# Reordering two small pieces of a matmul-bound kernel: a PSUM copy ahead of a gelu, and weight sums made form by form

## The chip, the cores and the metric

The kernel runs on one core of a Trainium2 chip. The metric is device time in microseconds (us), lower is better. The trace is one execution, taken by the hardware profiler; its span is about 1.7 us shorter than the time that is measured for the same execution.

Engines: PE is TensorE's matmul, PEld its weight load, DVE is VectorE, ACT is ScalarE, POOL is GpSimd, SP here only issues DMAs. PSUM is the memory in whose banks the matmuls accumulate. The granted clock is the share of TensorE's full clock that the trace records (1.00 is full, 0.50 is half). `L927` is line 927 of the kernel that the profile belongs to.

## The reference

```python
x = A_x                                             # 2048 x 1024
g = sigmoid((x * gate_w).sum(-1, keepdims=True))
a = A_ref(x, A_wqkv, A_wo)      # 32 heads of 32; each query sees 8 keys, at distance 0, 2, .. 14
b = B_ref(x, w_gate, w_up, w_down)                  # (gelu(x w_gate) * (x w_up)) w_down, 3584 wide
return g * a + (1 - g) * b
```

All arrays are bf16. `gelu` is the tanh approximation.

Of the kernel before, what the change touches and what calls it, by code (L numbers as in the profile page):

```python
# [136 lines left out]
def kernel(  # L137
# [19 lines left out]
    KH = KT // 2  # L157
# [55 lines left out]
    def tt(n, f32=False):  # L213
        return 0.07 + n / (960.0 if f32 else 1920.0)
# [25 lines left out]
    def ring_take(key):  # L240
        held[key] = ring_free.pop(0)[0]
        return ring[:, held[key], :]
# [278 lines left out]
    def qkv_forms():  # L521
        for sup in range(1, NSUP):
            c = 2 * sup
            t = tt(D // 2)
            for which in range(3):
                def g3(key):
                    return ring[:, held[key], :].rearrange("p (m t) -> p m t", t=NT)

                def raw(kt, hi, which=which, c=c):
                    return g3(("wqkv", c, which, kt))[:, :, KH * hi:KH * hi + KH]  # L530

                def form(f, kt, which=which, c=c):
                    return ring[:, held["wqf", c, which, f, kt // 2], kt % 2 * D // 2:(kt % 2 + 1) * D // 2] \
                        .rearrange("p (m t) -> p m t", t=KH)

                for k0 in range(0, KH, 2):
                    for f in (0, 2, 1, 3):
                        for kt in (k0, k0 + 1):
                            def go(f=f, kt=kt, which=which, c=c):
                                if f != 2 and kt % 2 == 0:  # L540
                                    ring_take(("wqf", c, which, f, kt // 2))
                                o, x_, y_, op = ((lambda: form(0, kt), lambda: raw(kt, 1), lambda: raw(kt + KH, 1), ALU.add),
                                                 (lambda: form(1, kt), lambda: form(0, kt), lambda: raw(kt, 0), ALU.subtract),
                                                 (lambda: raw(kt, 1), lambda: raw(kt, 0), lambda: raw(kt, 1), ALU.subtract),
                                                 (lambda: form(3, kt), lambda: raw(kt + KH, 0), lambda: form(1, kt),
                                                  ALU.subtract))[f]
                                V(out=o(), in0=x_(), in1=y_(), op=op)  # L547
                            dep = [("wqkv", c, which, kt), ("wqkv", c, which, kt + KH)]
                            if f in (1, 2):
                                dep.append(("wq", c, which, 0, kt))  # L550
                            elif f == 3:
                                dep.append(("wq", c, which, 1, kt))
                            yield dve(t, go, dep, key=("wq", c, which, f, kt), lag=0.5,
                                      pre=ring_pre if (f != 2 and kt % 2 == 0) else None)
# [365 lines left out]
    def ffn(sup, mid):  # L920
        T3, B22, B11, B21 = xr[:, 0], xr[:, 1], xr[:, 2], xr[:, 3]
        T1, T2, T4 = tf[:, 0], tf[:, 1], tf[:, 2]

        def mm(bk, form, rhs, f, start):
            wv, fl = piece(("w", sup, f // FB, form), KH), f % FB
            for k in range(KH):
                nc.tensor.matmul(banks[bk][:], lhsT=wv[:, k, fl * P:(fl + 1) * P], rhs=rhs[:, k, :],  # L927
                                 start=(start and k == 0), stop=(k == KH - 1), skip_group_check=True)

        def prod(bk, form, rhs, f, start, deps):  # L930
            b = f // FB
            o = pe(KH, lambda: mm(bk, form, rhs, f, start), [("w", sup, b, form)] + [x_ for x_ in deps if x_ is not None])
            yield o
            if f % FB == FB - 1:
                if sup == 0 and NSUP > 1 and not isinstance(form, str):
                    ring_give(("w", sup, b, form), o, w.done[("ws", b, form)])
                else:
                    ring_give(("w", sup, b, form), o)
            return o

        A, Bk, Dk, m5, u2, gl, ev = {}, {}, {}, {}, {}, {}, {}
        xf = [("xf", sup)]

        def hs(f, half):
            return hT[:, (1 - half) * NST:(2 - half) * NST, f, :]

        def v3(ap):
            return ap.rearrange("p (j s) -> p j s", s=P)

        for i in range(FT + 2):  # L950
            if i < FT:
                f = i
                A[f], fr = bank_take()
                o = yield from prod(A[f], "A11", B11, f, True, [fr] + xf)
                Bk[f], fr = bank_take()
                ev[f, "seed"] = act(0.5, lambda f=f: nc.scalar.copy(out=banks[Bk[f]][:], in_=banks[A[f]][:]), [o, fr] if fr else [o])  # L956
                yield ev[f, "seed"]
            if i >= FT:
                yield from mid[i - FT]
            if i >= 2:  # L960
                f = i - 2
                o = yield from prod(Bk[f], "A22", T4, f, False, [ev[f, "up2"]])
                e = act(0.48, lambda f=f: nc.scalar.copy(out=hs(f, 0), in_=v3(banks[Bk[f]][:])), [o])  # L963
                yield e
                bank_give(Bk[f], e)
                yield dve(tt(2 * SC), lambda f=f: nc.vector.tensor_tensor(  # L966
                    out=hT[:, :, f, :], in0=hT[:, :, f, :], in1=gl[f][:].rearrange("p (j s) -> p j s", s=P), op=ALU.mult),
                    [e, ev[f, "g1"], ev[f, "g2"]], key=("h", sup, f))
            if i < FT:
                f = i  # L970
                Dk[f], fr = bank_take()
                o = yield from prod(Dk[f], 0, T1, f, True, [fr])

                def cp(f=f):
                    m5[f] = work.tile([P, SC], F32, tag="m5", bufs=2, name="m5")
                    nc.scalar.copy(out=m5[f][:], in_=banks[Dk[f]][:])
                ev[f, "m5"] = act(0.48, cp, [o])
                yield ev[f, "m5"]
            if 1 <= i < FT + 1:
                f = i - 1  # L980
                o = yield from prod(Bk[f], 2, T3, f, False, [ev[f, "u2"]])
                d = [("stored", "o")] if (sup == 0 and f >= 8) else []
                if sup and f >= FT - NT:
                    d = [("qkv", 2 * sup + 1, 0, 0)]
                ev[f, "up2"] = dve(tt(SC, True), lambda f=f: nc.vector.tensor_tensor(
                    out=hs(f, 1), in0=v3(banks[Bk[f]][:]), in1=v3(m5[f][:]), op=ALU.add), [o, ev[f, "m5"]] + d)
                yield ev[f, "up2"]
            if i < FT:
                f = i
                o = yield from prod(A[f], "A12", B21, f, False, [ev[f, "seed"]])  # L990

                def g1(f=f):
                    gl[f] = work.tile([P, 2 * SC], BF16, tag="gl", bufs=3, name="gl")
                    nc.scalar.activation(out=gl[f][:, SC:2 * SC], in_=banks[A[f]][:], func=ACT.Gelu_apprx_tanh)  # L994
                ev[f, "g1"] = act(0.52, g1, [o], table="gelu")
                yield ev[f, "g1"]
                bank_give(A[f], ev[f, "g1"])
                o = yield from prod(Bk[f], 1, T2, f, False, [ev[f, "seed"]])

                def cp2(f=f):  # L1000
                    u2[f] = work.tile([P, SC], F32, tag="u2", bufs=2, name="u2")
                    nc.scalar.copy(out=u2[f][:], in_=banks[Bk[f]][:])  # L1002
                ev[f, "u2"] = act(0.48, cp2, [o])
                yield ev[f, "u2"]
                o = yield from prod(Dk[f], 3, B22, f, False, [ev[f, "m5"]])
                e = dve(tt(SC, True), lambda f=f: nc.vector.tensor_tensor(out=u2[f][:], in0=banks[Dk[f]][:],  # L1006
                                                                          in1=u2[f][:], op=ALU.add), [o, ev[f, "u2"]])
                yield e
                bank_give(Dk[f], e)
                ev[f, "g2"] = act(0.54, lambda f=f: nc.scalar.activation(out=gl[f][:, 0:SC], in_=u2[f][:],  # L1010
                                                                         func=ACT.Gelu_apprx_tanh), [e], table="gelu")
                yield ev[f, "g2"]
        w.done[("ffn", sup)] = o

    def down(c):
# [214 lines left out]
```

## The kernel before: what the change and the argument touch

The matmuls (qkv of the second half, gate/up, down) are made from seven products of half-sized blocks instead of eight (Strassen-Winograd). That needs sums of the weights and of x, made on VectorE ("forms"), and accumulators that are copied from one PSUM bank to another on ScalarE before more products are added to the copy (the "seed").

Instructions are not written in engine order by hand. Several Python generators ("streams") each yield operations in their own order, and a small list scheduler emits, again and again, the head that could start first by its own estimate of costs and of DMA landing times. On each engine, **the order of emission is the order of execution** (the trace before shows what that does: ScalarE stood idle for 3.82 us up to 102.91 before a gelu whose input was late, with the data of the seed copy emitted behind it ready):

```python
def _start(self, op):
    ...
    for d in deps:
        t = max(t, d.end + (0.04 if d.eng == op.eng else self.LAT + op.lag))
    return t
...
w.run([(0.0, main()), (0.0, loads()), (0.1, wforms()), (0.1, x_forms()), (0.1, qkv_forms()),
       (0.15, preps()), (0.3, attention()), (0.5, scores())])   # smallest estimate + bias goes first
```

The gate/up stage, one turn per block f of 128 columns (cut to its PE products and ACT copies, in order):

```python
for i in range(FT + 2):
    A11(i)      -> bank A                       # PE, 4 matmuls each
    seed(i):    bank Bk <- bank A               # ACT copy, L956
    A22(i-2)    -> Bk ; cast hT(i-2) <- Bk      # ACT, L963 ; DVE: hT *= gelu, L966
    form0(i)    -> Dk ; m5(i) <- Dk             # ACT copy, L976
    form2(i-1)  -> Bk ; DVE hT <- Bk + m5       # L985
    A12(i)      -> A  (needs seed(i)) ; g1(i) = gelu(A)     # ACT, L994
    form1(i)    -> Bk ; u2(i) <- Bk             # ACT, L1002
    form3(i)    -> Dk (needs m5(i)) ; DVE u2 <- Dk + u2     # L1006
    g2(i) = gelu(u2)                            # ACT, L1010, then the next turn's A11
```

The sums of the second qkv weights (16 for each of q, k, v; four forms times four row blocks):

```python
for k0 in range(0, KH, 2):          # rows 0,1 first, then rows 2,3
    for f in (0, 2, 1, 3):
        for kt in (k0, k0 + 1):
            yield dve(t, go, dep, key=("wq", c, which, f, kt), lag=0.5, ...)   # L547
```

PE uses them in the order: a product of raw weights, form 0 (all four rows, for two output blocks), form 1, raw, form 2, form 3, raw.

## Time and profile before

| | before |
|---|---|
| time, median of 3 | 745.33 us (744.88 to 747.23) |
| span of the traced execution | 744.5 us |
| PE busy | 727.6 us, 98% |
| DVE busy | 630.8 us, 85% (nearly gapless from 90 to 330) |
| ACT busy | 318.6 us, 43% |

First part of the page of the kernel before: busy us, share of the span, instructions.

```profile
PE 727.6 (98%) x3365; PEld 357.7 (48%) x3365; DVE 630.8 (85%) x931; ACT 318.6 (43%) x535; POOL 71.2 (10%) x123
```

PE is busy 98%, so only PE's waits can be won by moving things. They are few, and a view lists them. Waits of PE in the kernel before: who waited for whom, us in total, times, longest.

```profile
PE ps L580 <- DVE ring L547: 6.2, 2, 5.9
PE ps L927 <- ACT ps L956: 3.5, 3, 2.8
PE ps L274 <- DVE hT L272: 1.2, 1, 1.2
PE ps L1066 <- DMA ring<-in_A_wo_dram: 1.0, 2, 0.6
```

The first line is the weight sums of q, the second the seed copies; these two are what the change is after.

Timeline of the kernel before around the longest seed wait: start us, length, engine, line, operation, then the number of instructions merged into the line, and in brackets the idle time before it and what ended it.

```profile
102.19 0.68 DVE L1006 TENSOR_TENSOR u<-ps,u 128x512 f32<-128x512 f32 x1
...
102.91 0.63 ACT L1010 ACTIVATE gl<-u 128x512 bf16<-128x512 f32 x1 [3.82 <-DVE u L1006]
...
103.44 0.58 ACT L956 COPY ps<-ps 128x512 f32<-128x512 f32 x1
...
104.08 1.02 PE L927 MATMUL ps<-xr,ring 128*128 128x512 bf16 x4 [2.80 <-ACT ps L956]
```

ACT stood idle for 3.82 us with the seed's data ready (its matmuls ended near 99.4), because the gelu stood first in its queue and waited for VectorE, which was in attention work until 102.2.

Timeline of the kernel before, VectorE around the longest wait, with PE's restart last.

```profile
328.15 2.10 DVE L547 TENSOR_TENSOR ring<-ring 128x512 bf16<-128x512 bf16 x6
...
331.00 1.22 DVE L448 TENSOR_TENSOR xr<-xr 128x2048 bf16<-128x2048 bf16 x1
...
332.99 1.22 DVE L449 TENSOR_TENSOR tf<-xr,tf 128x2048 bf16<-128x2048 bf16 x1
334.13 3.10 DVE L547 TENSOR_TENSOR ring<-ring 128x512 bf16<-128x512 bf16 x9
...
334.94 4.76 PE L580 MATMUL ps<-tf,ring 128*128 128x512 bf16 x14 [5.90 <-DVE ring L547]
```

With one that ran at 326.55, seven sums are done by 330.2, but only two of the four rows of form 0 are among them. Two transposes for the gate (L690, 0.71 us each, among the lines left out) and two differences of x (L448, L449) stand before rows 2 and 3. Read also the last line's length: 14 matmuls took 4.76 us, where 216 ns apart they take 3.0 (the spacing of an undisturbed stretch of this trace: 8 in 1.89 us at 326.26, of which the last takes 0.38).

### The profile page before, as it was taken

The numbers are of one execution on the slowest core, as the hardware profiler recorded it, in microseconds if no ns is written. First come the engines' busy times: TensorE is split into PE (matmuls) and PEld (weight loads), VectorE is DVE, ScalarE is ACT, GpSimd is POOL, SyncE is SP. The second block draws the span as 40 slices with busy tenths as digits, with TensorE's granted clock in tenths as the row PEclk, the third lists the DMA queues.
The fourth block names the chain that finished last, engine by engine and source line by source line (L and its number), as shares of the span: only waits on it lengthen the run. The fifth ranks groups of instructions, "written<-read, shape, count | busy, mean of one in ns | idle before, by whom it ended". The sixth has DMA issues, their size and how long they took to land. (4 is left out here: it accounts for less than half of the span.)

```text
span 744.5 us, 9889 instructions
## 1 busy us (share of the span) xinstructions
PE 727.6 (98%) x3365; PEld 357.7 (48%) x3365; DVE 630.8 (85%) x931; ACT 318.6 (43%) x535; POOL 71.2 (10%) x123
## 2 busy tenths in 40 slices
PE   8999989999999999969999999999999999999997
PEld 5666634444444444435655444444444444444443
DVE  2789999999999999996999999999999997894300
ACT  2333445558555561016453121575566556210110
POOL 1234422121212000010000001000000000001000
PEclk9999999999999999999999999999999999999999
DMA  9999955655555459970234999855464645899983
GB/s 305 329 323 361 378 169 155 184 169 181 164 180 176 155 180 326 312 266 28 85 114 142 313 308 327 247 148 162 135 174 125 181 130 170 267 304 327 331 288 122
DMA packets 150435, 162.68 MB, mean 219 GB/s; under 512 B 22896, under 2 KB 110960, under 8 KB 150384
## 3 DMA queue, kind: packets, MB, share of 16 engines
q1 hardware_dynamic: 141552, 134.25, 58.7%
q0 software_dynamic: 8544, 27.27, 10.2%
q8 instruction: 26, 0.43, 0.2%
q10 hardware_dynamic: 288, 0.52, 0.2%
q14 instruction: 25, 0.20, 0.1%
HBM read 129.50 MB, written 28.31 MB: 212 GB/s over the span
## 5 line engine op out<-in xcount | busy, mean ns | idle before, releaser
L927 PEld LDWEIGHTS <-ring 128*128 128x128 bf16 x1568 | 153.4, 98 | 189.4 <-issue 5.1
L927 PE MATMUL ps<-xr,ring 128*128 128x512 bf16 x896 | 213.2, 379 | 3.5 <-ACT ps L956 3.5
L927 PE MATMUL ps<-tf,ring 128*128 128x512 bf16 x672 | 164.0, 379 | 0.0
L1066 PE MATMUL ps<-ring,hT 128*128 128x512 bf16 x708 | 160.6, 379 | 0.0
L1066 PEld LDWEIGHTS <-hT 128*128 128x128 bf16 x708 | 69.2, 98 | 83.5
L740 DVE TENSOR_TENSOR xbuf<-qo,kT 128x2048 bf16<-128x2048 bf16 x64 | 77.2, 1216 | 2.1 <-ACT kT L486 2.1
L879 DVE TENSOR_TENSOR xbuf<-xbuf,vT 128x2048 bf16<-128x2048 bf16 x64 | 77.4, 1217 | 0.2
L746 DVE TENSOR_TENSOR xbuf<-xbuf 128x2048 bf16<-128x2048 bf16 x56 | 68.1, 1216 | 0.2
L580 PEld LDWEIGHTS <-ring 128*128 128x128 bf16 x336 | 44.0, 131 | 36.6 <-DVE ring L547 7.2
L1010 ACT ACTIVATE gl<-u 128x512 bf16<-128x512 f32 x56 | 35.3, 631 | 61.0 <-DVE u L1006 61.0
L1101 ACT ACTIVATE ost<-ps,omg 128x512 bf16<-128x512 f32 x16 | 11.0, 687 | 115.0 <-PE ps L1066 115.0
L464 PE MATMUL ps<-xr,ring 128*128 128x512 bf16 x256 | 55.6, 379 | 0.3 <-DVE xr L1168 0.3
L1093 POOL DMA_DIRECT2D out_dram<-ost x24 | 13.0, 540 | 435.2 <-ACT ost L1101 340.8
L994 ACT ACTIVATE gl<-ps 128x512 bf16<-128x512 f32 x56 | 33.4, 597 | 47.9 <-PE ps L927 46.6
L1066 PE MATMUL ps<-ring,qo 128*128 128x512 bf16 x192 | 49.8, 379 | 1.2 <-DMA ring<-in_A_wo_dram 1.0
L464 PEld LDWEIGHTS <-ring 128*128 128x128 bf16 x256 | 36.7, 144 | 18.8 <-issue 0.4
L1006 DVE TENSOR_TENSOR u<-ps,u 128x512 f32<-128x512 f32 x56 | 38.4, 686 | 6.7 <-PE ps L927 3.6
L966 DVE TENSOR_TENSOR hT<-hT,gl 128x1024 bf16<-128x1024 bf16 x56 | 38.3, 684 | 6.3 <-ACT hT L963 6.1
L580 PE MATMUL ps<-xr,ring 128*128 128x512 bf16 x192 | 43.4, 379 | 0.0
L433 POOL DMA_DIRECT2D fforms<-ring x56 | 30.4, 544 | 126.0 <-DVE ring L425 115.9
L887 DVE TENSOR_TENSOR xbuf<-xbuf 128x1024 bf16<-128x1024 bf16 x64 | 41.8, 684 | 0.4
L580 PE MATMUL ps<-tf,ring 128*128 128x512 bf16 x144 | 35.0, 392 | 6.2 <-DVE ring L547 6.2
(101 smaller groups left out, 735.0 us busy)
## 6 DMA issues: line engine op xcount, KB each, us to landing
ring<-dforms SPq DMA_DIRECT2D x112, 256.0 KB, 4.7
ring<-in_B_w_down_dram SPq DMA_DIRECT2D x84, 256.0 KB, 4.1
ring<-in_B_w_gate_dram SPq DMA_DIRECT2D x56, 256.0 KB, 5.0
fforms<-ring POOLq DMA_DIRECT2D x56, 256.0 KB, 4.2
ring<-fforms SPq DMA_DIRECT2D x56, 256.0 KB, 3.7
ring<-in_B_w_up_dram SPq DMA_DIRECT2D x42, 256.0 KB, 3.9
ring<-in_A_wqkv_dram SPq DMA_DIRECT2D x40, 256.0 KB, 5.8
ring<-oforms SPq DMA_DIRECT2D x32, 256.0 KB, 5.6
```

The costliest lines, as they stand in the source:

```text
L464: nc.tensor.matmul(banks[bk][:], lhsT=lhsT, rhs=xT(c, kt), start=(kt == 0), stop=(kt == KT - 1))
L580: nc.tensor.matmul(banks[bk][:], lhsT=lhsT, rhs=rhs[:, kt, :], start=(start and kt == 0), stop=(kt == KH - 1), skip_group_check=True)
L740: V(out=w3(box[t]), in0=q_b, in1=k_w, op=ALU.mult)
L746: V(out=w3(box[0]), in0=w3(box[0]), in1=w3(box[t]), op=ALU.add)
L879: return dve(tt(n), taking(("p", t), lambda: V(out=w3(box["p", t]), in0=w3(box["ab"]), in1=v_w, op=ALU.mult)), [("qkv", c, 2, t), abo] + ( ...
L887: V(out=s4(t)[:, t % 2], in0=w3(box["p", t])[:, 0:4], in1=w3(box["p", t])[:, 4:8], op=ALU.add)
L927: nc.tensor.matmul(banks[bk][:], lhsT=wv[:, k, fl * P:(fl + 1) * P], rhs=rhs[:, k, :], start=(start and k == 0), stop=(k == KH - 1), skip_ ...
L966: yield dve(tt(2 * SC), lambda f=f: nc.vector.tensor_tensor(out=hT[:, :, f, :], in0=hT[:, :, f, :], in1=gl[f][:].rearrange("p (j s) -> p j ...
L994: nc.scalar.activation(out=gl[f][:, SC:2 * SC], in_=banks[A[f]][:], func=ACT.Gelu_apprx_tanh)
L1006: e = dve(tt(SC, True), lambda f=f: nc.vector.tensor_tensor(out=u2[f][:], in0=banks[Dk[f]][:], in1=u2[f][:], op=ALU.add), [o, ev[f, "u2"]])
L1010: ev[f, "g2"] = act(0.54, lambda f=f: nc.scalar.activation(out=gl[f][:, 0:SC], in_=u2[f][:], func=ACT.Gelu_apprx_tanh), [e], table="gelu")
L1066: nc.tensor.matmul(banks[bk][:], lhsT=l, rhs=wv[:, i, :], start=(start and k == 0), stop=(q == last and i == 1), skip_group_check=True)
```

## The change

Its intent: (1) let the seed of the next turn pass the gelu that waits for VectorE; (2) finish form 0 for all rows before any other form, in the order in which PE uses them. No work is added or removed.

```diff
-                for k0 in range(0, KH, 2):
-                    for f in (0, 2, 1, 3):
-                        for kt in (k0, k0 + 1):
+                for f in range(4):
+                    for kt in range(KH):
+                        if True:
                             def go(f=f, kt=kt, which=which, c=c):
 ...
-        xf = [("xf", sup)]
+        xf, late = [("xf", sup)], []
 ...
                 yield ev[f, "seed"]
+            while late:
+                yield late.pop(0)
             if i >= FT:
 ...
                 ev[f, "g2"] = act(0.54, lambda f=f: nc.scalar.activation(... Gelu_apprx_tanh), [e], table="gelu")
-                yield ev[f, "g2"]
+                late.append(ev[f, "g2"])
```

## The prediction

> What bounds it now. The page's first part gives TensorE (PE) 727.6 of 744.5 us busy, VectorE 631, ScalarE 319. So only PE's waits can be won. The view of PE's waits lists, after the start, 6.2 us for VectorE's sums of qkv weights (two waits, longest 5.9), 3.5 us for ScalarE's seed copies (2.8, 0.5, 0.2) and 1.0 us for a DMA. The rest is launch and tail, untouched.
>
> Seed copy part. It adds and removes nothing: the 631 ns gelu moves behind the next 579 ns seed copy. The timeline shows the 2.8 us wait at 101.3-104.1: VectorE reached the gelu's input only at 102.19, the gelu ran 102.91-103.5, then the seed, although the seed's own matmuls had ended near 99.4. After the change the seed is ready by 100, but the copy of the next product (the m5 buffer), still behind the gelu, ends near 104.1, where PE would need it at 103.0. I expect some 1.1 us of the stall to come back there: 1.7 us won. At 559.9 the 0.5 us wait (gelu behind an exp and two 1.28 us table loads) should vanish whole. The 0.2 us one belongs to a first seed, with no gelu ahead: stays. Side effect: the cast into hT comes up to 0.6 us later where the gelu used to be early; VectorE may idle a little before the multiply with the gelu. It is not bounding except near 324.
>
> Weight sums part. Same 16 sums (417 ns, 350 apart) for each of q, k, v, in another order. Timeline, 326-335: VectorE has been without a gap since about 275. It does seven sums (two rows of forms 0, 2, 1 and one of form 3) by 330.2, then two gate transposes and two 1.22 us differences of x, and only at 334.5-335.3 form 0 of rows 2 and 3, for which PE waits. Putting form 0 of all rows first would seem to remove all 6 us. I don't expect that. VectorE's order is fixed when the program is emitted, on estimated landing times; rows 2 and 3 of the weights are expected later than rows 0 and 1. So I expect row 2's form 0 ahead of the gate's transposes, one attention difference (0.65 us) slipped in before it, and row 3's form 0 still behind the two x differences, near 333.5-334. PE's stall shrinks from 5.9 to about 4.3 us. After today's stall 14 matmuls take 4.76 us instead of 14 x 0.216 = 3.0, at a granted clock of 0.6[...] half of 1.7 us expected. Weights of k and v: PE doesn't wait for them today, and should not after.
>
> Sum: 1.7 + 0.5 + 1.4 + 0.8 = 4.4 us less, provided that VectorE, which waits for PE now and then between 100 and 275, inherits PE's 1.7 us lead; else the second stall grows by it. Prediction 741.2 us, range 738.3 to 744.6. Chances: faster by over 2% 0.02, within 2% 0.96, slower 0.02.
>
> Right if: PE's waits show no seed wait over 0.3 us, one about 1 us wait for the m5 copy or none; the wait for the weight sums is 3-5 us, behind the last x difference; all busy times are unchanged within 0.5%. Wrong if: the weight sum wait disappears (then 736-738), or the forms of k and v become a wait, or a late cast delays VectorE in the first half so that the wait near 330 doesn't shrink (744-746).

The last term, 0.8 us, is the author's estimate: half of the about 1.7 us by which the 14 matmuls after the 5.9 us stall (4.76 us in the trace of the kernel before) exceed 3.0.

## More of the kernel before

The change adds two lines, so lines after 957 move down by two in the changed kernel (the gelu L1010 is L1012 there, the m5 copy L976 is L978).

A load's estimated end is that of a single pipe of 340 GB/s, plus 2.2 us. Both are constants in the scheduler's code (`RATE` and the line that sets a load's end), not measurements; the page of the kernel before has up to 378 GB/s in one of its 20 slices and medians of 3.7 to 5.8 us from issue to landing in the lines that it lists.

## The result, and the profile after

| | before | after |
|---|---|---|
| time, median of 4 | 745.8 us (744.88 to 747.23) | 741.23 us (740.83 to 741.6) |
| span of the traced execution | 744.5 | 739.1 |
| PE waits for seeds | 3.5 us | none listed |
| PE waits for the m5 copy | none | 3.1 us, two of 1.5 |
| PE waits for weight sums | 6.2 us | 1.6 us |

The ratio is 0.9937, 95% interval 0.9919 to 0.9955. Here and below a ratio is the mean time of one kernel's runs over that of the other's of the same rounds, so it is not quite the ratio of the medians. Executions over 1.5% slower than the fastest of the same kernel are left out of the means. The output is correct.

The time is the predicted one to 0.03 us, and the parts are not. Waits of PE in the changed kernel:

```profile
PE ps L927 <- ACT m L978: 3.1, 2, 1.5
PE ps L580 <- DVE ring L547: 1.6, 1, 1.6
PE ps L274 <- DVE hT L272: 1.2, 1, 1.2
```

The seed waits are gone, but nearly as much came back as waits for the m5 copy. Timeline of the changed kernel, the place that answers to 102-104 above:

```profile
100.65 0.57 ACT L956 COPY ps<-ps 128x512 f32<-128x512 f32 x1 [0.55 <-PE ps L927]
...
102.54 0.57 ACT L978 COPY m<-ps 128x512 f32<-128x512 f32 x1
...
102.99 1.03 PE L927 MATMUL ps<-tf,ring 128*128 128x512 bf16 x4
```

The seed now runs at 100.65, as soon as its matmuls end, and PE does not stop. The m5 copy that I expected to be late ends at 103.1, in time: VectorE reached the gelu's input (L1008) 6.1 us after the stage's first matmul (101.29 against 95.21), before the change 8.0 us after it (102.19 against 94.19). This distance isn't the change's doing: two experiments below that keep the old order here (sums_only and filler) have 5.7 and 7.8 us, so it differs between executions, and with it the wait. The two m5 waits lie elsewhere. Timeline of the changed kernel before the first of them, ScalarE alone and, last, PE (the second, at 550, has the same sequence):

```profile
255.79 1.28 ACT L703 ACT_TABLE_LOAD   x1
257.09 0.22 ACT L703 ACTIVATE ez<-zc 128x16 f32<-128x16 f32 x1
257.21 0.58 ACT L956 COPY ps<-ps 128x512 f32<-128x512 f32 x1
257.81 1.28 ACT L1012 ACT_TABLE_LOAD   x1
259.10 0.63 ACT L1012 ACTIVATE gl<-u 128x512 bf16<-128x512 f32 x1
...
260.22 1.28 ACT L838 ACT_TABLE_LOAD   x1
261.52 0.63 ACT L838 ACTIVATE xbuf<-xbuf 128x512 f32<-128x512 f32 x1
262.05 0.57 ACT L978 COPY m<-ps 128x512 f32<-128x512 f32 x1
...
262.67 1.02 PE L927 MATMUL ps<-xr,ring 128*128 128x512 bf16 x4 [1.53 <-ACT m L978]
```

The gelu stands between two exps (the gate's at 257.09 and the attention's at 261.52), so the function table is loaded three times here and, for the gelu after it, once more. A load takes 1283 ns (the mean of each line's), and the whole switch at 255.79 took 1.3 us: the copy before it ended at 255.78, the exp began at 257.09. The m5 copy waits behind all of it. Over the whole kernel the table is loaded 18 times, before 16 times.

Timeline of the changed kernel, VectorE at the weight sums and PE's restart:

```profile
326.17 0.36 DVE L547 TENSOR_TENSOR ring<-ring 128x512 bf16<-128x512 bf16 x1
326.44 0.70 DVE L690 STREAM_TRANSPOSE zt<-ps 128x512 f32<-128x512 f32 x1
...
329.24 1.22 DVE L449 TENSOR_TENSOR tf<-xr,tf 128x2048 bf16<-128x2048 bf16 x1
330.38 4.44 DVE L547 TENSOR_TENSOR ring<-ring 128x512 bf16<-128x512 bf16 x13
...
331.10 2.75 PE L580 MATMUL ps<-tf,ring 128*128 128x512 bf16 x12 [1.60 <-DVE ring L547]
```

The order is the predicted one: row 2's form 0 (326.17) stands before the transposes, row 3's (the first of the 13) behind the last difference of x. But it happens over 3 us earlier than I had put it: row 3's at 330.4, not 333.5 to 334. And the matmuls after the wait are not slow: 12 in 2.75 us. So VectorE reached this place much earlier, though nothing was taken from its work. The experiments had to find which half of the change did that.

### The profile page after: what moved, and what is told of

It is laid out like the page before. It is cut to its first block, busy times and chain, and to the rows that moved or that the text cites. A ratio compares the mean times of both kernels' runs of the same rounds, so it can differ in the third digit from the quotient of the medians.

```text
span 739.1 us, 9823 instructions
## 1 busy us (share of the span) xinstructions
PE 723.0 (98%) x3298; PEld 358.0 (48%) x3365; DVE 630.6 (85%) x931; ACT 321.6 (44%) x537; POOL 71.2 (10%) x123
## 4 chain that ended last, share of the span: by engine, by line
PE 86%; DVE 7%; DMA 2%; ACT 2%; issue 2%; DVEq 0%; ACTq 0%
PE ps L927 44%; PE ps L1068 21%; PE ps L464 11%; PE ps L580 9%; DVE xbuf L879 1%; DMA ring<-dforms 1%; DVE xbuf L887 1%; DVE xbuf L746 1%; DMA ring<-fforms 1%; DVE hT L1036 1%; DVE xbuf L740 0%; DMA hT<-in_A_x_dram 0%; PE ps L685 0%; PE ps L1163 0%; DVE tf L1036 0%
## 5 line engine op out<-in xcount | busy, mean ns | idle before, releaser
L927 PE MATMUL ps<-tf,ring 128*128 128x512 bf16 x659 | 162.6, 379 | 0.8
L956 ACT COPY ps<-ps 128x512 f32<-128x512 f32 x56 | 32.1, 573 | 52.9 <-PE ps L927 52.9
L1008 DVE TENSOR_TENSOR u<-ps,u 128x512 f32<-128x512 f32 x56 | 38.4, 686 | 5.9 <-PE ps L927 2.7
L987 DVE TENSOR_TENSOR hT<-ps,m 128x512 bf16<-128x512 f32 x56 | 38.5, 687 | 3.0 <-PE ps L927 2.6
```

Of the source, the lines that this page charges most:

```text
L927: nc.tensor.matmul(banks[bk][:], lhsT=wv[:, k, fl * P:(fl + 1) * P], rhs=rhs[:, k, :], start=(start and k == 0), stop=(k == KH - 1), skip_ ...
L987: ev[f, "up2"] = dve(tt(SC, True), lambda f=f: nc.vector.tensor_tensor(out=hs(f, 1), in0=v3(banks[Bk[f]][:]), in1=v3(m5[f][:]), op=ALU.add ...
L1008: e = dve(tt(SC, True), lambda f=f: nc.vector.tensor_tensor(out=u2[f][:], in0=banks[Dk[f]][:], in1=u2[f][:], op=ALU.add), [o, ev[f, "u2"]])
```

## Experiments

All results were correct. The first four below ran on one chip, the others on a second. Times are medians of fast runs.

### The two halves alone

The sums' order alone, seeds as before; and the seeds alone, sums' order as before. Each is the diff above with the other half left out. The changed kernel ran again beside them.

> The changed kernel again, beside its two halves. Repeat of 0.9937, 0.992 to 0.996; PE waits 1.6 us for the weight sums and twice 1.5 us for the m5 copy, none for a seed.

> Only the new order of the weight sums. My theory (VectorE stands where it stood before, row 3's form 0 is still behind both x differences, as predicted): seed waits 2.8, 0.5 and 0.2 stay, the sums' wait goes from 5.9 to about 4.3 us, ratio 0.997 to 0.999. Rival A (the order of the sums alone makes the big gain): the wait falls below 2 us and the ratio is at or below 0.995.

> Only the seed copies ahead of the gelu. My theory after seeing the result: no seed wait over 0.3 us, but two new 1.5 us waits for the m5 copy, and VectorE earlier against PE near 325, so the sums' wait falls too, to 2 to 3.5 us, though the sums' order is the old one; ratio 0.994 to 0.997. Rival A: the sums' wait stays near 6 us and the ratio is 0.998 or more.

The last column is PE's time from its first raw product of q to the first product behind form 0, 24 matmuls; without a stop they took 5.18 us (the run `landing` below).

| | median us | ratio to before (95%) | sums' wait | m5 waits | seed waits | PE's form-0 stretch |
|---|---|---|---|---|---|---|
| before (waits and stretch: its trace, as above) | 746.16 | 1 | 6.2 | 0 | 3.5 | 13.27 |
| both (after_again) | 740.45 | 0.9929 (0.9915 to 0.9943) | 2.4 | 3.1 | 0 | 9.39 |
| sums_only | 744.62 | 0.9984 (0.9971 to 0.9997) | 5.2, longest 3.9 | 0 | 1.6 | 13.26 |
| seed_only | 742.64 | 0.9953 (0.9936 to 0.9970) | 3.2 | 3.1 | 0 | 8.67 |

The weight sums' order alone measured 1.5 us (0.2 to 2.2 us by the interval). Its profile has the order that the prediction drew: longest wait 3.9 us (predicted about 4.3), row 3 behind the x differences. But I had expected the seed waits of 2.8, 0.5 and 0.2 us to stay, and that missed. The long one is 0.5 us here, and the restart at the sums is as slow as before. Timeline of sums_only, both places:

```profile
102.56 1.02 PE L927 MATMUL ps<-xr,ring 128*128 128x512 bf16 x4 [0.54 <-ACT ps L956]
...
332.33 5.27 PE L580 MATMUL ps<-tf,ring 128*128 128x512 bf16 x13 [3.86 <-DVE ring L547]
```

Up to the sums VectorE has the same order in both kernels, so the seed wait alone differs by 2.3 us between executions. At the sums nothing was gained in this trace: the stretch took 13.26 us, before 13.27, as slower matmuls followed the shorter stall (13 in 5.27 us). So how much of the 1.5 us the sums' order wins is not shown.

The seeds alone are worth 3.5 us, although their own waits net to almost nothing (3.5 us taken away, 3.1 us of m5 waits put in their place). The gain is at the *other* wait: the sums' wait fell from 6.2 to 3.2 us with the sums' order untouched, and the matmuls behind it kept the full clock, so the stretch took 8.67 us instead of 13.27.

Why? Busy time of each engine between 90 and 320 us, in the kernel before, in sums_only and in seed_only (columns: stretch, its length, then busy us and instructions of PE, PEld, DVE, ACT, POOL, the granted clock, DMA share, GB/s):

```profile
90.00:320.00 230.00, 226.03 (x1045) 102.39 (x1044) 222.41 (x311) 115.82 (x194) 31.58 (x57) 1.00 0.67 201
```

```profile
90.00:320.00 230.00, 228.60 (x1057) 103.91 (x1056) 222.48 (x311) 116.29 (x194) 31.70 (x58) 1.00 0.67 203
```

```profile
90.00:320.00 230.00, 227.19 (x1049) 103.07 (x1048) 224.60 (x314) 116.13 (x194) 32.08 (x58) 1.00 0.67 201
```

The third busy time is VectorE's. With the seeds ahead it does 224.6 us of work in these 230 us, without them 222.4. It waits 2.2 us less. The large transpose of the attention half that precedes the sums (L803) began at 319.4 in sums_only and 315.9 in the changed kernel. Its lines in the kernel before and in seed_only:

```profile
320.88 2.30 DVE L803 STREAM_TRANSPOSE xbuf<-xbuf 128x2048 bf16<-128x2048 bf16 x1
```

```profile
315.42 2.30 DVE L803 STREAM_TRANSPOSE xbuf<-xbuf 128x2048 bf16<-128x2048 bf16 x1
```

The two groups don't overlap: 314.8 to 316.1 in the six usable traces with the gelu moved and the exps (below) left alone, 319.4 to 322.8 in the three with the old order of the seeds (filler is the third). So the seed half moved VectorE ahead by about 5 us at this place. In seed_only it is 5.5 us. VectorE was idle for 27.7 us up to the transpose instead of 31.3; 0.7 of these 3.6 us lie before 62 us, ahead of this stage's first seed (95 us), and are chance. Another 0.7 us is one output operation that now stands behind the transpose. All the other instructions before it are the same in number and kind; they were busy 1.1 us less.

### The slow matmuls after a stall

After the 5.9 us stall of the kernel before, matmuls came 430 ns apart for about 3.3 us. I filled that stall with 20 repeats of one matmul whose result is overwritten.

```diff
                 for kt in range(KH):
 ...
+                    if which == 0 and t == 0 and form == 0 and kt == 0:
+                        for _ in range(20):
+                            nc.tensor.matmul(banks[bk][:], lhsT=lhsT, rhs=rhs[:, kt, :], start=True, stop=False, ...)
```

> The kernel before with 20 repeats of one matmul (4.3 us of PE work, overwritten) put into its 5.9 us stall. If the slow matmuls after the stall (14 in 4.76 us) are the cost of a clock halved by the idle time, the stall's end stays at the same sum and the time falls by 1.5 to 1.9 us: ratio 0.9975 to 0.998. If those matmuls are slow because they wait for the following sums one by one, ratio 0.9995 to 1.0005.

Measured: 744.91 us, ratio 0.9988 (0.9968 to 1.0008), single runs from 743.23 to 748.41. The ratio is inconclusive. In the profile a wait of 2.3 us was left, and after it 14 matmuls took 5.01 us: the clock fell all the same. But this execution is the slowest of the six and the only one with a mean granted clock of 0.995; the others have 0.998 to 1.000, while all 33 executions of the kernel before that ran beside the experiments have 0.993 to 0.995. So the filler kept more of the clock in most executions; the two at 1.000 took 743.23 and 743.74 us.

The changed kernel has 1.000 in six of its ten executions (739.96 to 740.86 us) and 0.997 or 0.998 in four (741.59 to 742.69), seed_only 1.000 in two of six, sums_only in none. So part of the change's gain is a clock that is lost less often. The profiles show single cases. Timeline lines of PE's restart at the sums, in after_again, seed_only and filler:

```profile
331.07 4.64 PE L580 MATMUL ps<-tf,ring 128*128 128x512 bf16 x13 [2.38 <-DVE ring L547]
```

```profile
331.12 3.33 PE L580 MATMUL ps<-tf,ring 128*128 128x512 bf16 x14 [3.18 <-DVE ring L547]
```

```profile
336.81 5.01 PE L584 MATMUL ps<-tf,ring 128*128 128x512 bf16 x14 [2.31 <-DVE ring L547]
```

The mean granted clock in the first 2 to 3 us after the restart was 0.50 in after_again, 1.00 in seed_only and 0.59 in filler. The *longer* idle time (3.18 us) kept the clock; the shorter ones (2.38 and 2.31 us) lost it. The changed kernel itself was caught both ways: 1.6 us of waiting and a clock of 1.00 afterwards (12 matmuls in 2.75 us) in one execution, 2.38 us and 0.50 (13 in 4.64 us) in another. At full clock 8 matmuls took 1.89 us and 24 took 5.34, so 13 take about 3.0 and the fall cost about 1.7 us. So in these traces the length of the idle time alone doesn't decide, and a wait of 2.31 us was enough for a fall. What decides is not shown.

### The gelu behind the m5 copy too

```diff
-            while late:            # was behind the seed
-                yield late.pop(0)
 ...
                 yield ev[f, "m5"]
+            while late:
+                yield late.pop(0)
```

> The changed kernel, with the late gelu put behind the m5 copy of the next product too. My theory (the two new 1.5 us waits come from the gelu and its table load standing ahead of the m5 copy): both vanish. The first of them, near 262, is paid back at the weight sums, whose wait grows by up to 1.5 us, because VectorE isn't helped; the second, near 550, is kept. Ratio 0.990 to 0.992. Rival: the waits come from the exp itself, stay, and the ratio is that of the changed kernel, 0.993.

> The run gelu_after_m5 again, because its profile fell into a slow execution. Its times equalled the changed kernel's (0.9928). Theory: the m5 waits of 3.1 us are down to under 1 us and the sums' wait is larger than the 1.6 to 2.4 us of the changed kernel, by 1 to 2 us, so the gain is paid back there. Rival: the m5 waits are still there.

Measured: 740.6 us, ratio 0.9928 (0.9915 to 0.9941), no gain over the changed kernel's 0.9929 and outside what I had expected. The profile of this run fell into an execution of 957.85 us at a mean granted clock of 0.754, whose cause is not known here, and is not used; the other five runs lie between 740.27 and 740.70. The second run gave 740.73 us and a usable profile. Its waits and its restart at the sums:

```profile
PE ps L580 <- DVE ring L547: 5.2, 2, 4.3
```

```profile
330.17 5.32 PE L580 MATMUL ps<-tf,ring 128*128 128x512 bf16 x12 [4.27 <-DVE ring L547]
```

Both m5 waits are gone, all 3.1 us, so they did come from the gelu and its table load in front of the copy. And the sums' wait is 5.2 us instead of 1.6 to 2.4, with slow matmuls behind it. Row 3's form 0 came at 329.3, 1.1 us earlier than in the changed kernel, and PE arrived still earlier (at 322.2 instead of 327.0 for the first raw product; 1.5 us of this is the m5 wait, 1.0 us an earlier start of the stage, the rest mostly fewer waits for DMAs). PE merely arrives earlier at a place where VectorE sets the time, and pays back there.

### The two exps side by side

The gate's small exp and the attention's exp become one operation of the scheduler, so that no gelu can fall between.

```diff
-        if a == 0:
-            yield from gate_exp(c)
-        e = act(0.55, lambda: nc.scalar.activation(out=lsb(), ... Exp, scale=scale), [o], table="exp", lag=0.6)
+        def exps():
+            if a == 0:
+                nc.scalar.activation(out=gates[c][0][:], in_=gates[c][2][:], func=ACT.Exp)
+            nc.scalar.activation(out=lsb(), ... Exp, scale=scale)
+        e = act(0.7 if a == 0 else 0.55, exps, [o] + ([("zc", c)] if a == 0 else []), table="exp",
+                lag=0.6, key=("ez", c) if a == 0 else None)
```

> The changed kernel, with the small exp of the gate emitted directly before the exp of the attention half, so that no gelu falls between and two table loads (2 x 1.28 us) are saved in each of the two stages. My theory: the two 1.5 us waits for the m5 copy fall below 0.5 us in sum, ratio 0.989 to 0.992. Rival: the table loads are not what holds the m5 copy, and the waits stay at 3 us in sum.

Measured: 742.64 us, ratio 0.9956 (0.9942 to 0.9969), slower than the changed kernel in after_again, with intervals that just touch. My expectation missed. The two m5 waits of 1.5 us are gone, and the table loads fell from 18 to 11, but one m5 wait of 0.9 us stands at 103, the place that the prediction had named. And the attention of VectorE slipped back: its transpose before the sums began at 320.4 (before 320.9, changed kernel 315.9), and the sums' wait was 6.5 us. Saving seven table loads of 1.28 us on an engine that is busy 43% bought nothing; what came with it is a new order on VectorE and a time that is 2 us longer.

### An earlier landing estimate for q's weights

This tests the prediction's step that the scheduler's *estimated* landing times keep row 3 of form 0 behind. Only the estimate changes; the semaphores that guard the data are set elsewhere and stay.

```diff
-                            yield dve(t, go, dep, key=("wq", c, which, f, kt), lag=0.5,
+                            yield dve(t, go, dep, key=("wq", c, which, f, kt), lag=0.5 if which else -3.0,
```

> The changed kernel, with the weights of q estimated to land 3.5 us earlier when the program is emitted; nothing else. Tests the step that VectorE's fixed order, made on estimated landing times, keeps row 3's form 0 behind the x differences. My theory: all four sums of form 0 stand ahead of the gate's transposes, the sums' wait is below 0.5 us, no slow matmuls after it, ratio 0.988 to 0.991. Rival (the weights really land late, or VectorE is simply behind): the wait stays at 1.5 us or more.

Measured: 738.29 us, ratio 0.9900 (0.9885 to 0.9915). PE's wait for the sums is gone from the list; the timeline of this kernel shows why:

```profile
324.73 2.43 DVE L547 TENSOR_TENSOR ring<-ring 128x512 bf16<-128x512 bf16 x7
...
326.91 3.62 PE L580 MATMUL ps<-tf,ring 128*128 128x512 bf16 x15
...
327.08 0.71 DVE L690 STREAM_TRANSPOSE zt<-ps 128x512 f32<-128x512 f32 x1
```

All of form 0 stands before the transposes, VectorE never waited for a weight, and PE passes without a stop at full clock. So the weights had landed by then; the estimate was what kept the sums back. A wait of 0.6 us for VectorE's addition of an output of q (L641), which the next product needs, turned up. The m5 waits stand at 3.6 us: the two of 1.5, and one where the prediction had put it. Timeline of this kernel:

```profile
103.49 1.89 PE L927 MATMUL ps<-xr,ring 128*128 128x512 bf16 x8 [0.50 <-ACT m L978]
```

### Together

> The three together. If the gains add: no seed, m5 or sums wait above 0.5 us, 735 to 737 us, ratio 0.985 to 0.988. If VectorE, which is busy nearly throughout the first 330 us, sets the pace, waits turn up elsewhere and the ratio is no better than that of the best of the three by more than 0.001.

> Earlier landing estimate plus late gelu behind the m5 copy, without the paired exps. With the sums' wait gone the m5 gain can't be paid back there: if the theory holds, 736 to 737.5 us, ratio 0.987 to 0.989, against 0.990 of the landing estimate alone. Rival: still 0.990, because the m5 waits are only moved.

> Earlier landing estimate plus paired exps, gelu where the change put it. The paired exps alone made the changed kernel 2 us slower, with the sums' wait at 6.5 us. If that was only VectorE arriving later at the sums, it costs less here, as the sums stand first: ratio 0.987 to 0.990. Rival: pairing is bad in itself, ratio 0.992 or more.

| on top of the changed kernel | median us | ratio to before (95%) |
|---|---|---|
| gelu behind m5 | 740.6 | 0.9928 (0.9915 to 0.9941) |
| exps side by side | 742.64 | 0.9956 (0.9942 to 0.9969) |
| earlier landing | 738.29 | 0.9900 (0.9885 to 0.9915) |
| earlier landing, gelu behind m5 | 736.09 | 0.9865 (0.9849 to 0.9882) |
| earlier landing, exps side by side | 738.72 | 0.9898 (0.9882 to 0.9915) |
| all three | 735.8 | 0.9867 (0.9849 to 0.9885) |

The changed kernel itself has 0.9929 (0.9915 to 0.9943), on the first chip. The gelu behind the m5 copy was worth nothing while the sums' wait stood, and 2.2 us once it was gone. It is the same edit, and it removed 3.1 us of m5 waits in the one case and 3.6 in the other: what decides is whether another engine sets the time further on. Pairing the exps adds nothing in any company; it doesn't hurt where the sums stand first. The version to keep has the two edits "earlier landing" and "gelu behind m5": 736.09 us, 1.3% better than the kernel before and better than the changed one. Its longest wait of PE:

```profile
PE ps L580 <- DVE qo L641: 1.5, 1, 1.5
```

## Why the prediction was right or wrong

- **The total was right**: 741.2 predicted, 741.23 measured, range and class too. In the repeat the gain was larger, 5.7 us (746.16 to 740.45). Part of this exactness is luck, as two terms of the sum were off in opposite directions.
- **Seed waits vanish, right.** Even the 0.2 us one, which I had said would stay, is not listed.
- **"Some 1.1 us of the stall to come back there" (near 103), right in mechanism, but not what took the gain.** In the profile of the changed kernel the m5 copy was in time there, as VectorE reached the gelu's input 6.1 us after the stage's first matmul. In landing it came 7.4 us after it and in exp_pair 7.9, and the wait is there, 0.5 and 0.9 us. The seed wait itself differs in the same way: 2.8 us in the kernel before, 0.5 in sums_only. So this term, worked out from one trace, hung on chance. Not foreseen were two waits of 1.5 us for the same copy at 262 and 550, where the gelu, moved behind the seed, fell between two exps and cost table loads. I looked at the three old waits only and did not ask where else the m5 copy would now stand behind a slow gelu. The seed part's own waits netted 0.4 us, not the 2.2 of the sum.
- **Sums' order, right in mechanism, its gain not shown.** "I don't expect that" (the whole 6 us) held. Alone it measured 1.5 us against a sum of 1.4 + 0.8, but its trace shows no gain at the sums (13.26 and 13.27 us) and a shorter seed wait. Row 2 ahead, row 3 behind the x differences, because of estimated landing times: seen in the order, and shown by changing nothing but the estimate.
- **The proviso, "VectorE ... inherits PE's 1.7 us lead", right in direction and too small.** VectorE gained about 5 us at that place. That is the term that was mis-sized: the sums' wait fell to 1.6 us (2.4 in the repeat), outside "3-5 us". It makes up for what the seed part lacked. seed_only shows that it belongs to the seed half. Why the emission order that the seeds brought about gives VectorE fewer waits was not taken apart further; that exp_pair, with the seeds still ahead, is back at 320.4 while PE is there 3.2 us earlier than in the kernel before (323.0 and 326.3), shows that PE being ahead is not enough: it hangs on the order.
- **Clock, half right.** The 0.8 us was an estimate. That the changed kernel, with its shorter stall (1.6 and 2.4 us in its two traces, 5.9 before), sometimes escapes the slow clock is what the runs show: six of its ten executions had 1.000, none of the 33 of the kernel before. That a shorter stall escapes it more often as a rule is not shown: 3.18 us kept the clock and 2.31 us lost it. The clock of 0.6 is the mean of a window that is mostly stall (0.61 from 330 to 336 us); behind the restart it was 0.50 to 0.56.
- **Busy times unchanged, nearly**: VectorE 630.8 and 630.6 us; ScalarE rose from 318.6 to 321.6 us, by 0.9% instead of the 0.5% that I had allowed, 2.6 us of it two more table loads. PE's busy time after the change can't be compared, as 67 of its 3365 matmul records are missing in that trace.

## What to carry to other kernels

When a wait on a nearly full engine is taken away, look down the same engine for the next place where another engine sets the time: there the gain is paid back, as the gelu behind m5 was (a sums' wait of 5.2 us instead of 1.6 to 2.4), or, as with the seeds, the larger part of the gain appears (3.2 us instead of 6.2). When an instruction moves back in an in-order queue, ask of every instruction that it now stands before (here a copy that PE needs, two waits of 1.5 us, and an exp that needs another function table, 1.28 us a load) what it will delay, everywhere in the kernel and not only at the wait that one wants to remove. Where a scheduler fixes an engine's order from estimates, a wrong estimate of a landing can be a wait (1.6 us for the sums in the changed kernel, none listed with the earlier estimate): compare it with the trace before moving work by hand.
